# A delta-rule attention block followed by a two-layer PReLU feed-forward, one core: VectorE's weight differences and block-inversion pieces of chunks two to four dealt out anew, and one step's late transposes issued one group earlier

## The chip, the cores and the metric

The kernel runs on one core of one Trainium2 chip. That core has five engines that run side by side, each taking its own instructions in order: TensorE (PE in the profile: matmuls and transposes; PEld is its weight load), VectorE (DVE), ScalarE (ACT), GpSimd (POOL) and SyncE (SP, which here only issues DMAs). Engines wait for one another through semaphores. The metric is the device time of one execution in microseconds (us); lower is better.

## The reference

Four batches, eight heads, 768 tokens, head size 48. For each head a 48 x 48 state runs over the tokens; its outputs, laid side by side, are the 384 inputs of a feed-forward with 2048 inner units.

```python
k_n = k / (np.linalg.norm(k, axis=-1, keepdims=True) + 1e-06)
for t in range(S):
    y[:, :, t] = einsum('bhd,bhde->bhe', q[:, :, t], state)
    v_old = einsum('bhde,bhd->bhe', state, k_n[:, :, t])
    state = state + beta[:, :, t] * einsum('bhd,bhe->bhde', k_n[:, :, t], v[:, :, t] - v_old)
x = y.transpose(0, 2, 1, 3).reshape(B * S, H * D)      # 3072 x 384
h = x @ w_in                                           # 384 -> 2048
g = np.maximum(h, 0.0) + alpha * np.minimum(h, 0.0)
out = g @ w_out                                        # 2048 -> 384
```

## The kernel before

**Chunks and steps.** The tokens are cut into 12 chunks of 64. A chunk holds 256 tokens over the four batches. The attention of one chunk is done in two *steps*, one for each pair of batches, so there are 24 steps, n = 0 to 23; step n belongs to chunk n // 2. Inside a chunk the recurrence is solved as a triangular system: a Gram matrix of the keys (`grams`, L495), the inverse of a unit triangular matrix, a product with the state (`through_state`, L793), the solve with the inverse (`solve`, L824, whose result `u` VectorE scales at L831), the outputs (`outputs`, L836) and the new state (`next_state`, L853).

**Block inversion.** The 32 x 32 diagonal blocks of four steps at a time are inverted together on VectorE by `eliminate` (L578). Such a job has 39 pieces (`WHOLE`, L619): four transposes in, one piece for GpSimd, 30 elimination pieces of one product (L593) and one addition (L599), and two times four transposes out (`back`, L605), of which the last four write `inverse`. ScalarE's `placing` (L693) puts the result where the step's matmuls read it (L704, L707). `between` (L749) makes the off-diagonal part on TensorE (L733), and ScalarE copies it back (L745).

**Feed-forward.** `ffn_in` (L989) makes the 2048 inner units of a chunk in eight groups of six matmuls (L998; each shows as two records in the trace). A group fills one PSUM bank; ScalarE takes the negative part out of it (L1008) and VectorE adds the scaled parts with two instructions (L1010), after which the bank is free. Up to step 8 there are only two such banks (`ps_ffn`, L101), so group i + 2 cannot begin before L1010 of group i has ended. From chunk 2 on the second layer is `ffn_out_fast` (L1051), a scheme with seven block products instead of eight (L1062). It needs four sums of the activations in each of two halves (`operand_sums`, L943, VectorE L952) and, once for the whole kernel, four differences of blocks of `w_out` in each of two halves: `weight_sums(b, first, last)` (L970), eight instructions of 128 x 768 values at L985. The first three differences of a half go to spare memory, the fourth overwrites a block of `w_out` itself and is needed only by the last of the seven products. The plain second layer of chunk 1, `ffn_out(1)` (L1028, matmuls L1041), still reads `w_out` as it was.

**Who orders the work.** Every engine's order is written out by hand. `weave` (L1376) takes generators, each with a number of pieces and a place from which it starts, and lets them advance in proportion; `part(g, n)` takes the next n pieces of a generator. Steps 4 and 5 are each one `weave` (L1913) of `attention(n)` in four groups, `part(late, rest)`, which is the rest of `ffn_out(1)`, and `part(blocks, share)`, pieces of the block inversion for steps 8 to 11. Step 5 also weaves in `weight_sums(0, 0, 3)`. From step 6 (`JOINED`) on a step is three `stretch`es of matmuls of the feed-forward (`tail`), woven with the block pieces that `PIECES_OF` (L1920) deals out and with the extra generators of `extra`. The other five weight differences stand in steps 6 and 7: `weight_sums(1, 0, 3)` in step 6's second stretch, `weight_sums(0, 3, 4)` in its third, `weight_sums(1, 3, 4)` in step 7's first.

**Step 4 and 5's groups.** Group 1 of `attention(n)` is `through_state`, a mask (L521), `between_1`; group 2 `solve`, `grams`, `between_2`; group 3 `outputs`, `next_state` and the squares of a later step's keys (ScalarE L388, VectorE L392); group 4 `flips` (L440), `to_ffn` (L901), the norm's root and reciprocal (ScalarE L407 and L408, VectorE L412) and loads. `flips` turns a later step's keys and queries round with eight TensorE transposes (L429) into a pair of PSUM banks, from which ScalarE copies them (L455, L457). `to_ffn` does the same with the step's outputs (L908, L910).

**Three PSUM pairs in turn.** `ps_big` (L77) hands out three pairs of banks round and round. So in step 5 `solve` reuses the pair of `through_state`, which the mask L521 reads last; `flips` reuses the pair of `between_2`, which the copies L745 read last; and step 6's `through_state` reuses the pair of `flips`, which L457 reads last.

Of the kernel before, what the change touches and what calls it, by code (L numbers as in the profile page):

```python
# [36 lines left out]
EARLY = 8  # L37
# [7 lines left out]
def kernel(  # L45
# [31 lines left out]
    def ps_big():  # L77

        big.append(big.pop(0))
        return big[-1]  # L80
# [313 lines left out]
    def squares(n):  # L394
        if n < N:
            squared(n)
            norms(n)
# [42 lines left out]
    def flips(n_k, n_q):  # L440

        both = n_k < N and n_q < N
        p = ps_big() if both else None
        copies = []
        if n_k < N:
            p_k = p[:, 0] if both else ps_one()
            flip(early(n_k), p_k)
            k_t[n_k] = work.tile([128, G, 128], FP32, name="k_t", bufs=EARLY + 1)
            copies.append((k_t[n_k], p_k))
        if n_q < N:  # L450
            p_q = p[:, 1] if both else ps_one()
            flip(q_pad[n_q % NQ], p_q)
            q_t[n_q] = beside[steps[n_q][1]][:, :, :, D : D + C]
        for dst, src in copies:
            nc.scalar.copy(dst.rearrange("p g i -> p (g i)")[0:ROWS], src[0:ROWS])  # L455
        if n_q < N:
            nc.scalar.copy(  # L457
                q_t[n_q].rearrange("p t g i -> p g t i")[0:ROWS],
                p_q.rearrange("p (g t i) -> p g t i", g=G, t=2)[0:ROWS],
            )  # L460
# [67 lines left out]
    NJ = 4  # L528
# [192 lines left out]
    PLACING = 3  # L721
# [246 lines left out]
    summed = []  # L968
# [82 lines left out]
    def ffn_out_fast(c):  # L1051


        gss.pop(c)
        later = operand_sums(1)
        o = [work.tile([128, DM], FP32, name="o_sb") for _ in range(2)]
        left, right_ = slice(0, DM // 2), slice(DM // 2, DM)
        u = [work.tile([128, DM // 2], FP32, name=f"u{i}", bufs=1) for i in (2, 3)]

        def some(p, x, w, which):  # L1060
            for i in which:
                nc.tensor.matmul(p, x(i), w(i), start=(i == 0), stop=(i == FP - 1))  # L1062
                if i % 2 == 1:
                    next(later, None)
                    if i < FP - 1:
                        yield

        def product(x, w):
            p = ps_ffn()[:, 0 : DM // 2]
            yield from some(p, x, w, range(FP))  # L1070
            return p

        def operand(f, u):
            return lambda i: act[:, i, f, u * 128 : (u + 1) * 128]

        def sum_(x):
            return lambda i: sums[:, i, x]

        def weight(f, v):
            return lambda i: w_half[:, i, f, v]  # L1080

        def w_sum_(x):
            return lambda i: w_sum(i, x)

        def add(to, x, p):
            nc.vector.tensor_tensor(out=to, in0=x, in1=p, op=ALU.add)

        if len(ffn_banks) > 2:
            a, b = (
                (ps_ffn()[:, 0 : DM // 2], operand(f, 0), weight(f, 0)) for f in range(2)  # L1090
            )
            yield from some(*a, range(FP - 2))
            yield from some(*b, range(FP - 2))
            yield from some(*a, range(FP - 2, FP))
            nc.scalar.copy(u[0], a[0])
            yield
            yield from some(*b, range(FP - 2, FP))
            add(o[0][:, left], u[0], b[0])
            yield
        else:  # L1100
            p = yield from product(operand(0, 0), weight(0, 0))
            nc.scalar.copy(u[0], p)
            yield
            p = yield from product(operand(1, 0), weight(1, 0))
            add(o[0][:, left], u[0], p)
            yield
        for _ in later:
            assert False
        assert summed.count(0) == summed.count(1) == 4
        p = yield from product(sum_(1), w_sum_(1))  # L1110
        add(u[0], u[0], p)
        yield
        p = yield from product(lambda i: act[:, i, 0, 128:256], w_sum_(2))
        add(u[1], u[0], p)
        yield
        p = yield from product(sum_(0), w_sum_(0))
        add(o[0][:, right_], u[0], p)
        add(o[1][:, right_], u[1], p)
        yield
        p = yield from product(sum_(2), weight(1, 1))  # L1120
        add(o[0][:, right_], o[0][:, right_], p)
        store(c, 0, o[0])
        yield
        p = yield from product(operand(1, 1), w_sum_(3))
        add(o[1][:, left], u[1], p)
        store(c, 1, o[1])
        yield
# [243 lines left out]
    def part(gen, n):  # L1371
        for _ in range(n):
            next(gen, None)
            yield
# [18 lines left out]
    def attention(n):  # L1393

        assert n + EARLY + 1 < TURNED_K
        now(through_state(n))
        now(between_1(n + 1))
        yield
        now(solve(n))
        now(grams(n + EARLY))  # L1400
        now(between_2(n + 1))
        scale_v(n + 1)
        yield
        now(outputs(n))
        now(next_state(n))
        load_late(n + 2)
        squares(n + EARLY + 1)
        yield
        flips(n + EARLY + 1, n + 2)
        to_ffn(n)  # L1410
        if n < JOINED - 1:
            place(n + 2, (0,))
        now(weigh(n + EARLY + 1))
        if n == JOINED - 1:
            load_early(TURNED_K)
        load_q(n + 3)
        load_v(n + 3)
        yield

    WY, JOINED = G * D, NJ + 2  # L1420
# [196 lines left out]
    n = 2 * W_IN_P  # L1617
# [16 lines left out]
    def chain(*gens):  # L1634
        for g in gens:
            yield from g
# [92 lines left out]
    n = 12  # L1729
# [114 lines left out]
    n = WHOLE + PIECES - BEGUN - SOON  # L1844
# [31 lines left out]
    n = OUT_PARTS - few - 2 * rest + 1  # L1876
# [30 lines left out]
        gens += [(part(blocks, share), share, 0.3), (each(later), len(later), soon)]  # L1907
        weave(*[x for x in gens if x[1] > 0])

    share = 9  # L1910
    for n in range(NJ, JOINED):
        extra = [] if n == NJ else [(weight_sums(0, 0, 3), 3)]
        weave(  # L1913
            (attention(n), SHARES), (placing(n + 1, (1, 2, 3)), SHARES * PLACING),
            (part(late, rest), rest),
            (part(blocks, share), share), *extra,
        )
# [11 lines left out]
    for n in range(JOINED, N):  # L1929
        if n == NARROW:  # L1930
            banks(2, 2)
        fill, share = FILL.get(n, FILLS[n % 2]), PIECES_OF.get(n, TURNS[n % NJ])
        extra = [[], [], []]
        if n == JOINED:
            place(n + 1, (0,))
            extra[1] = [(weight_sums(1, 0, 3), 3)]
            extra[2] = [(weight_sums(0, 3, 4), 1)]
        elif n == JOINED + 1:
            extra[0] = [(weight_sums(1, 3, 4), 1, 0.6), (placing(n + 1, (1, 2, 3)), PLACING)]

        later = burst_a(n)
        if is_turned(n - 1):
            if n % 2:
                rows = rows_y(n - 1)
                extra[1].append((part(rows, 8), 8))
                extra[2].append((part(rows, 8), 8, 0.3))
            else:
                extra[0].append((rows_y(n - 1), 16, 0.4))
        stretch(
            fill[0], blocks, share[0], later, *extra[0], *put_off, soon=0.5 if n == JOINED else 0.0  # L1950
        )
        put_off = []
        later = turn_round(n)
        if n == JOINED:
            extra[1].append((placing(n + 1, (1, 2, 3)), PLACING))
        stretch(fill[1], blocks, share[1], later, *extra[1], soon=0.2)
        m, ends = (n + 6) // NJ, n % NJ == 2
        if ends and n > JOINED:
            for _ in blocks:
                assert False  # L1960
            place(n + 2, (0,))
        later = burst_b(n) + [lambda: scale_v(n + 1)]
        if NARROW <= n < N - 2:
            later.append(lambda: turn_q(n + 2))
        if n == JOINED:
            stretch(fill[2], blocks, share[2], later, *extra[2])
            for _ in blocks:
                assert False
            place(n + 2, (0,))
            place(n + 3, (0,))  # L1970
            blocks = eliminate(m)
        else:
            if ends:
                blocks = eliminate(m) if m < N // NJ else iter(())
            after = [(placing(n + 2, (1, 2, 3)), PLACING)]
            if n % NJ != 1:
                after.append((placing(n + 3, (0,)), 1))
            if n >= LATE:
                put_off, after = after, []
            stretch(  # L1980
                fill[2], blocks, share[2], later, *after, *extra[2], soon=0.1 if n >= LATE else 0.5
            )
# [34 lines left out]
```

## Time and profile before

| what | value |
| --- | --- |
| three runs | 643.0 us median (642.51 to 644.19) |
| profiled execution, its own time | 643.5 us |
| span of the profile | 641.8 us |
| granted TensorE clock | 1.0 of full speed |
| PE busy over 155 to 208 us | close to all of it, with five waits listed |
| weight differences L985 | 8 x 0.95 us, at 165.0, 169.9, 173.6, 183.0, 185.7, 187.6, 190.7 and 202.1 us |

Rows of the timeline read: start (us from the span's start), duration (us), engine, line, operation, output<-input, size, count, and in brackets how long the engine had been idle and what released it. Two neighbouring rows may overlap: an engine starts the next instruction while the former still drains. So the distance from one start to the next is what a row costs on its engine. A row with a count merges several instructions.

Steps stand in this profile at about these times: step 4 from 146 us, step 5 from 160, step 6 from 173.5, step 7 from 194.5, step 8 from 219.

### The profile page before, as it was taken

The numbers are of one execution on the slowest core, as the hardware profiler recorded it, in microseconds if no ns is written. First come the engines' busy times: TensorE is split into PE (matmuls) and PEld (weight loads), VectorE is DVE, ScalarE is ACT, GpSimd is POOL, SyncE is SP. The second block draws the span as 40 slices with busy tenths as digits, with TensorE's granted clock in tenths as the row PEclk, the third lists the DMA queues.
The fourth block names the chain that finished last, engine by engine and source line by source line (L and its number), as shares of the span: only waits on it lengthen the run. The fifth ranks groups of instructions, "written<-read, shape, count | busy, mean of one in ns | idle before, by whom it ended". The sixth has DMA issues, their size and how long they took to land.

```text
span 641.8 us, 21687 instructions
## 1 busy us (share of the span) xinstructions
PE 627.9 (98%) x9154; PEld 552.0 (86%) x9154; DVE 500.8 (78%) x1213; ACT 309.9 (48%) x816; POOL 92.4 (14%) x204
## 2 busy tenths in 40 slices
PE   6999999999999999999999999999999999999997
PEld 4587887566787988988988988988999999999997
DVE  4976988977999889859879858968979569477383
ACT  5887664344454243644643735435447356353230
POOL 6001211000000100001000000000044053061350
PEclk9999999999999999999999999999999999999999
DMA  7957835311343143143143122121121310100000
GB/s 118 300 129 167 237 66 141 82 28 37 56 77 57 30 74 53 27 77 52 26 75 52 25 50 31 33 45 26 32 47 27 54 26 6 36 1 2 26 1 26
DMA packets 145969, 39.27 MB, mean 61 GB/s; under 512 B 139040, under 2 KB 142256, under 8 KB 145872
## 3 DMA queue, kind: packets, MB, share of 16 engines
q1 hardware_dynamic: 144000, 37.40, 28.5%
q8 instruction: 72, 1.18, 0.7%
q10 hardware_dynamic: 1872, 0.49, 0.4%
q14 instruction: 25, 0.20, 0.1%
HBM read 33.14 MB, written 4.72 MB: 59 GB/s over the span
## 4 chain that ended last, share of the span: by engine, by line
PE 82%; DVE 10%; ACT 2%; DMA 2%; issue 1%; SPq 1%; POOL 1%; ACTq 0%; DVEq 0%; POOLq 0%
PE p_ffn L998 11%; PE p_ffn L1062 9%; PE p_more L1331 8%; PE p_more L1062 8%; PE p_more L998 7%; PE p_ffn L1041 7%; PE p_more L1247 4%; PE p_ffn L1237 3%; PE p_ffn L1331 3%; PE p_ffn L1242 2%; PE p_pair L733 2%; PE p_pair L802 2%; PE p_pair L1508 2%; PE p_pair L840 2%; PE p_pair L501 2%; DVE act L1010 2%
## 5 line engine op out<-in xcount | busy, mean ns | idle before, releaser
L998 PE MATMUL p_ffn<-xt,w_in 128*128 128x256 f32 x528 | 124.1, 384 | 1.3 <-ACT space_out L263 0.4
L998 PEld LDWEIGHTS p_ffn<-xt,w_in 128*128 128x128 f32 x528 | 97.4, 190 | 16.3 <-issue 1.6
L896 ACT COPY xt<-z 32x96 f32<-32x96 f32 x240 | 64.5, 269 | 48.5 <-DVE z L883 45.4
L998 PE MATMUL p_more<-xt,w_in 128*128 128x256 f32 x240 | 55.7, 382 | 0.0
L599 DVE TENSOR_TENSOR block<-block,prod 128x30 f32<-128x30 f32 (+9 forms) x150 | 49.8, 332 | 5.2
L1271 POOL TENSOR_TENSOR k_t<-k_t 128x128 f32<-128x128 f32 (+1 forms) x48 | 28.3, 590 | 166.6 <-ACT k_t L1266 164.1
L998 PEld LDWEIGHTS p_more<-xt,w_in 128*128 128x128 f32 x240 | 44.9, 190 | 6.3
L745 ACT COPY inv<-p_pair 32x256 f32<-32x256 f32 x40 | 14.5, 363 | 73.4 <-DVE u L831 40.9
L593 DVE TENSOR_TENSOR prod<-block 128x30 f32<-128x30 f32 (+9 forms) x150 | 48.7, 325 | 1.1
L418 POOL TENSOR_TENSOR beta_t<-beta_t,rec 128x8 f32<-128x8 f32 x24 | 6.1, 255 | 271.0 <-DVE rec L412 262.0
L1010 DVE SCALAR_TENSOR_TENSOR act<-act,al_t,p_ffn 128x256 f32<-128x256 f32 x72 | 31.1, 473 | 15.9 <-ACT act L1008 15.8
L1008 ACT ACTIVATE act<-p_ffn 128x512 f32<-128x512 f32 x36 | 21.4, 594 | 28.3 <-PE p_ffn L998 28.0
L1271 POOL TENSOR_TENSOR block<-block 128x128 f32<-128x128 f32 (+1 forms) x48 | 27.6, 575 | 12.6 <-ACT block L1266 10.1
L1237 PE MATMUL p_ffn<-xt,w_in 128*128 128x256 f32 x96 | 29.3, 387 | 0.0
L1062 PE MATMUL p_ffn<-w_out,act 128*128 128x192 f32 x160 | 28.4, 329 | 0.5 <-DVE act L1010 0.4
L1062 PEld LDWEIGHTS p_ffn<-w_out,act 128*128 128x128 f32 x160 | 26.2, 190 | 1.7 <-DVE act L1010 0.8
L831 DVE TENSOR_TENSOR u<-p_pair,wgt 128x384 f32<-128x384 f32 x24 | 13.2, 554 | 16.6 <-PE p_pair L827 10.1
L1010 DVE SCALAR_TENSOR_TENSOR act<-act,al_t,p_more 128x256 f32<-128x256 f32 x40 | 17.3, 474 | 10.9 <-ACT act L1008 10.8
L812 DVE TENSOR_TENSOR r<-v_raw,p_pair 64x192 f32<-64x192 f32 (+1 forms) x66 | 23.2, 352 | 2.3 <-PE p_pair L802 1.2
L554 ACT COPY same<-right 32x256 f32<-32x256 f32 x29 | 11.7, 402 | 22.7 <-DVE right L507 19.1
L1062 PE MATMUL p_more<-w_out,act 128*128 128x192 f32 x128 | 22.3, 326 | 0.0
L1041 PE MATMUL p_ffn<-w_out,act 128*128 128x384 f32 x64 | 21.8, 491 | 0.4 <-DVE more L1010 0.4
(256 smaller groups left out, 1472.8 us busy)
## 6 DMA issues: line engine op xcount, KB each, us to landing
w_out<-in_moe_w_in_dram SPq DMA_DIRECT2D x10, 512.0 KB, 5.3
v_raw<-in_v_dram SPq DMA_DIRECT2D x48, 96.0 KB, 2.7
kl<-in_k_dram SPq DMA_DIRECT2D x96, 48.0 KB, 2.5
out_dram<-o_sb SPq DMA_DIRECT2D x90, 48.0 KB, 1.6
space_out<-in_moe_w_out_dram SPq DMA_DIRECT2D x11, 384.0 KB, 4.3
ke_last<-in_k_dram SPq DMA_DIRECT2D x25, 96.0 KB, 3.3
qp<-in_q_dram SPq DMA_DIRECT2D x64, 32.0 KB, 2.2
w_out<-in_moe_w_out_dram SPq DMA_DIRECT2D x5, 384.0 KB, 4.3
```

What stands on the lines that cost most here:

```text
L593: nc.vector.tensor_tensor(out=prod, in0=r[:, 0:j, j : j + 1].to_broadcast([128, j, n]), in1=r[:, j : j + 1, j + 1 : HB].to_broadcast([128, ...
L599: nc.vector.tensor_tensor(out=r[:, 0:j, j + 1 : HB], in0=r[:, 0:j, j + 1 : HB], in1=prod, op=ALU.add)
L812: nc.vector.tensor_tensor(out=r[to, a], in0=v_in[to, a], in1=p[own, a, :, 0:D], op=ALU.subtract)
L896: nc.scalar.copy(to[quad(r), u, bp, t], z[quad(2 * t + u), r])
L998: nc.tensor.matmul(p_h[:, i], w_in[:, t, (f + i) * 128 : (f + i + 1) * 128], xt[:, t], start=(t == 0), stop=(t == KT - 1),)
L1010: nc.vector.scalar_tensor_tensor(out=g[:, i], in0=g[:, i], scalar=al_t[:, f + i : f + i + 1], in1=p_h[:, i], op0=ALU.mult, op1=ALU.add,)
L1041: nc.tensor.matmul(p_o[u], gs[f // 2][:, f % 2, u * 128 : (u + 1) * 128], w_out[:, f], start=(f == 0), stop=(f == FT - 1),)
L1062: nc.tensor.matmul(p, x(i), w(i), start=(i == 0), stop=(i == FP - 1))
L1237: nc.tensor.matmul(p[:, f * 256 : f * 256 + 256], w(2, f), xt[:, 2], start=True, stop=False)
L1247: nc.tensor.matmul(q[:, j], a, b, start=True, stop=True)
L1271: nc.gpsimd.tensor_tensor(out=dst, in0=a, in1=b, op=ALU.add)
L1331: nc.tensor.matmul(p, x(i), w(i), start=(i == 0), stop=(i == FP - 1))
```

## The change

Four edits. Line numbers in this document are those of the kernel before.

1. The three differences `weight_sums(0, 0, 3)` move from step 5 to step 4.
2. `share`, the block pieces of steps 4 and 5, goes from 9 to 10 in each. The number of pieces in step 6's second stretch is worked out from `share`, and falls from 4 to 2.
3. `weight_sums(1, 0, 3)` begins in the first stretch of step 6 with one difference and has its other two in the second. The two last differences, of both halves, move into the third stretch of step 7. An assertion in `ffn_out_fast` that all eight have been issued moves behind the first products accordingly.
4. In step 5 alone `flips` is issued with group 3, ahead of the `yield`, and not with group 4. Between the two groups stand three matmuls of `ffn_out(1)`.

```diff
@@ ffn_out_fast
-        assert summed.count(0) == summed.count(1) == 4
+        assert summed.count(0) >= 3 and summed.count(1) >= 3
         p = yield from product(sum_(1), w_sum_(1))
...
+        assert summed.count(0) == summed.count(1) == 4
         p = yield from product(operand(1, 1), w_sum_(3))
@@ attention
         squares(n + EARLY + 1)
+        if n == JOINED - 1:
+            flips(n + EARLY + 1, n + 2)
         yield
-        flips(n + EARLY + 1, n + 2)
+        if n < JOINED - 1:
+            flips(n + EARLY + 1, n + 2)
         to_ffn(n)
@@ steps 4 and 5
-    share = 9
+    share = 10
     for n in range(NJ, JOINED):
-        extra = [] if n == NJ else [(weight_sums(0, 0, 3), 3)]
+        extra = [(weight_sums(0, 0, 3), 3)] if n == NJ else []
@@ steps 6 and 7
         if n == JOINED:
             place(n + 1, (0,))
-            extra[1] = [(weight_sums(1, 0, 3), 3)]
-            extra[2] = [(weight_sums(0, 3, 4), 1)]
+            own = weight_sums(1, 0, 3)
+            extra[0] = [(part(own, 1), 1, 0.5)]
+            extra[1] = [(part(own, 2), 2)]
         elif n == JOINED + 1:
-            extra[0] = [(weight_sums(1, 3, 4), 1, 0.6), (placing(n + 1, (1, 2, 3)), PLACING)]
+            extra[0] = [(placing(n + 1, (1, 2, 3)), PLACING)]
+            extra[2] = [(chain(weight_sums(0, 3, 4), weight_sums(1, 3, 4)), 2)]
```

Set side by side, the two built programs hold the same instructions on every engine. ScalarE, GpSimd and SyncE have them in the same order. On TensorE one thing moves: the eight transposes of step 5's `flips` stand ahead of three matmuls L1041 that they followed. On VectorE the order differs from step 4's sixth elimination piece to the second elimination piece of the next block inversion, which stands at 214.3 us in the profile before:

| place on VectorE | before | after |
| --- | --- | --- |
| step 4 | 9 pieces of the block inversion | 10 pieces, three L985 |
| step 5 | 9 pieces, three L985 | 10 pieces |
| step 6, from L507's end to the first L1010 | 2 pieces | 2 pieces, one L985 |
| step 6, from there to the fourth L1010 | 4 pieces, three L985 and the first that overwrites `w_out` | 3 pieces, two L985 |
| step 7, ahead of the mask L521 | the second L985 that overwrites `w_out` | none |
| step 7, from L507's end to the third elimination piece of the next block inversion | none | both L985 that overwrite `w_out` |

## The prediction

> **What bounds the kernel now.** I read the page first: its first part and the chain that ended last.
>
> ```profile
> PE 627.9 (98%) x9154; PEld 552.0 (86%) x9154; DVE 500.8 (78%) x1213; ACT 309.9 (48%) x816; POOL 92.4 (14%) x204
> ...
> PE 82%; DVE 10%; ACT 2%; DMA 2%; issue 1%; SPq 1%; POOL 1%; ACTq 0%; DVEq 0%; POOLq 0%
> ```
>
> TensorE sets the end; VectorE holds only a tenth of the chain. In the chain by time that tenth lies mostly at 184 to 207 and 237 to 257 us; the diff touches 150 to 214 us. So I read TensorE's timeline there, and the chain for its pace when nothing is late.
>
> ```profile
> 289.15 5.18 PE p_more L998 x24
> ```
> ```profile
> 172.66 0.81 PE L1041 MATMUL p_ffn<-w_out,more 128*128 128x384 f32 x2
> 173.66 1.00 PE L802 MATMUL p_pair<-beside,k_t 48*64 48x112 f32 x32 [0.19 <-ACT beside L457]
> ...
> 180.36 1.89 PE L998 MATMUL p_ffn<-xt,w_in 128*128 128x256 f32 x8
> 182.69 3.88 PE L998 MATMUL p_ffn<-xt,w_in 128*128 128x256 f32 x16 [0.43 <-DVE act L1010]
> 186.50 0.69 PE L501 MATMUL p_pair<-k_t 48*64 48x64 f32 x32
> ...
> 196.63 4.58 PE L998 MATMUL p_ffn<-xt,w_in 128*128 128x256 f32 x20
> 201.76 0.55 PE L908 MATMUL p_pair<-ident,y 128*128 128x128 f32 x3 [0.54 <-ACT mid L745]
> 202.14 2.76 PE L998 MATMUL p_ffn<-xt,w_in 128*128 128x256 f32 x12
> 205.14 2.51 PE L1062 MATMUL p_ffn<-w_out,act 128*128 128x192 f32 x14 [0.24 <-DVE act L1010]
> 207.82 1.96 PE L1062 MATMUL p_ffn<-w_out,act 128*128 128x192 f32 x10 [0.17 <-DVE act L1010]
> ```
>
> The bracketed idle times add to 1.57 us. I price by starts instead, since the ends are modelled. L998 at full pace costs 5.18 / 24 = 0.216 us, L1062 0.1625 (the chain's 5.20 for 32), L1041 0.34 (six from 169.41 to 171.45 in the same timeline); a run that follows or precedes small matmuls costs about 0.1 more at that end.
>
> - A: 182.69 and the rest to 186.50: 6.14 us for 24 L998 against 5.18 + 0.09: 0.87 lost.
> - B: 201.76: 5.13 for 20 against 4.32 + 0.2: 0.6.
> - C: 205.14: 3.00 for 12 against 2.59: 0.4.
> - D: 207.82: 2.68 for 14 against 2.28: 0.4.
> - E: 173.66: 1.00 for two L1041 against 0.7: 0.3.
>
> Together 2.57 us. That is all the change can win here. A, C and D wait for VectorE's L1010; B for ScalarE, which had itself waited for VectorE:
>
> ```profile
> 198.78 0.51 ACT L704 ACTIVATE inv<-inverse,which 128x256 f32<-128x256 f32 x1 [3.04 <-DVE inverse L566]
> ...
> 200.96 0.74 ACT L745 COPY mid<-p_pair 32x256 f32<-32x256 f32 x2
> ```
>
> The Trainium skill ("Trainium Kernel Development and Optimization", Performance Expectations, "Reading a trace") calls matmul busy time a bad metric, as matmuls are pipelined. The rows agree: 1.57 by idle, 2.57 by starts. By idle alone the sum below would be 641.8.
>
> **Part 1: three L985 and one piece into step 4.** VectorE had room there:
>
> ```profile
> 155.25 0.55 DVE L849 TENSOR_TENSOR y<-y,p_pair 128x384 f32<-128x384 f32 x1 [0.55 <-PE p_pair L840]
> ...
> 160.84 0.20 DVE L412 RECIPROCAL rec<-norm 128x8 f32<-128x8 f32 x1 [2.47 <-ACT norm L408]
> ...
> 165.02 0.95 DVE L985 TENSOR_TENSOR space_out<-w_out 128x768 f32<-128x768 f32 x1
> 165.89 0.40 DVE L593 TENSOR_TENSOR prod<-block 128x240 f32<-128x240 f32 x1
> ```
>
> An L985 costs 0.87 from start to start. A piece's addition is followed 0.44 later by the next piece, which needs it, but 0.32 later by an independent row (164.70 to 165.02), so each L985 between two pieces costs about 0.77. Laying the new order over the old starts: `u` (L831) 151.48 to 152.27 (TensorE's L840 needs it at 154.50), L849 155.25 to 156.25 (L908 at 158.50), then 867 and 392, two pieces, the third L985 at 159.29, the extra piece, and L412 at 160.86 instead of 160.84. The room of 3.02 is used up to the last 0.02. Cost 0.02, and none to spare: behind L412 stand L812 and the mask L521 of step 5, and the solve already waits for that mask:
>
> ```profile
> 164.40 0.56 PEld L827 LDWEIGHTS p_pair<-r,inv 64*64 64x64 f32 x32 [0.60 <-DVE a_t L521]
> ```
>
> Every us that VectorE comes later to L412 is a us of TensorE at L827. Bounds: VectorE 0.3 earlier gains 0.06 (the L1041 before it hide the rest); 0.3 later costs 0.3. I take 0.02.
>
> The skill ("VectorE: DVE Perf Modes", Terms, DRAIN) says the next VectorE operation cannot issue until the pipe is empty. The rows disagree: the piece behind the L985 starts 0.08 before its recorded end. By the rule the three would cost 0.24 more, and the sum 641.1.
>
> **Part 2: step 5 without L985.** Behind the mask two L985 (1.6) leave ahead of `right` (L507) or L849, and a piece (0.8) comes: L831 167.54 to 166.8, L507 168.33 to 167.6, L849 171.49 to 170.0.
>
> **Part 3: `flips` one group earlier.** Eight L429, no DMA of their own; their keys and queries landed long before (issues at 124 and 159.4 to 161.7, landing 3.7 at most). They move past three L1041 (2.04), to 169.41. Their banks are free only when `between_2`'s L745 has ended: before at 170.35, behind L554, which waited for L507. With L507 0.73 earlier L745 ends at 169.62. So TensorE, which runs through at 169.41 before, waits about 0.26; bounds: 0 (L507 1 us earlier) and 0.94 (not earlier at all). Behind the wait stand the three L1041 and L908, which nobody misses. In return L457 ends near 171.7, two us ahead of L802, and E goes: -0.3. Step 5 as a whole: +0.02 + 0.26 - 0.3, nothing. The loads that wait for L429 on SyncE's queue come no later.
>
> **Part 4: step 6.** L412 now waits for the norm (174.05 against 175.17) and L812 to L507 run 1.1 earlier. L554 starts at 178.1 (179.24), L388 and the first L1008 at 179.5 (180.62), and the first L1010 ends at 181.3 (182.46), with one L985 ahead of it. TensorE wants the bank at 182.1. The second ends at 184.0 (185.3), wanted at 184.75; its L466 needs `qp`, whose last issue at 179.0 lands by 182.7 at most, at the end of the L985. The third ends at 186.5 (189.3). A goes whole: -0.87.
>
> From L831 on VectorE keeps up with TensorE and so gains no more by waiting: the fourth L1010 at 190.1 (191.64). The rest follows at the old spacing, so the last transpose of `inverse` ends at 197.15 (198.74). L704, the next L1008 (TensorE's group ends 197.8) and four copies put L745's end at 200.36 (201.70), and L908 wants it at 200.3: of B's 0.6 some 0.1 stays. -0.5. Bounds: 0 to -0.6.
>
> **Part 5: step 7 without the second `w_out` L985.** The next L1010 stands at 201.7 (204.13) against a need at 203.4; the last at 204.9 (207.32), its first half done 205.3 against 205.7. C and D go: -0.8; bounds -0.4 (only C) and -0.8.
>
> **Where the two L985 land.** 0.87 each between 211 and 214 us. Ahead of the first L1086 (213.42 to 212.7, with all else earlier) and the second (215.67 to 213.9). What covers them: before, VectorE was idle 0.94 at 215.67, and TensorE needs the bank that the first L1086 frees only at about 213.3. Cover gone, each costs at most its 0.87.
>
> **Sum.** 0 - 0.87 - 0.5 - 0.8 = -2.2 us. The profiled execution took 643.5 (span 641.8, 1.7 around it), half a us over the median, which is inside the runs' spread; I subtract from the median: 643.0 - 2.2 = **640.8**. Behind 214 us TensorE's order is the same and VectorE has idle spots to fall back in step, so I carry the gain to the end.
>
> **The rivals.** About 0.3% (1.9 us) is what a measurement of this kernel can tell from no change.
>
> - *Half of it is given back in step 5.* VectorE's chain in step 4 is 0.4 longer than I laid it: L827 waits 0.4, L507 comes 0.3 earlier only and `flips` waits 0.65, and B stays with 0.3. -2.2 + 0.4 + 0.4 + 0.2 = -1.2: 641.8. For: the margin of 0.02 comes from eight added starts. Against: those are rows of the same shapes. 0.27.
> - *The wait for the norm stays (slower).* L412 before waited 2.47 for ScalarE. If ScalarE's root comes late by as much as VectorE's L392 (157.24 instead of 156.24) and what then stands before it, VectorE is idle again with the L985 already spent: 2.9 late at L412 and so at L827. Less the later gains of 2.2 and plus 0.3 at `flips`: 644.0. It decides once L412 starts after 163. Against: L407 started at 160.33, 2.6 after L392's new end, held by L455 to L707 and not by L392. 0.06.
> - *It does nothing:* the waits at A to D are only moved to other groups of the same two banks, since PSUM turn-over and not VectorE's load sets them: 642.7. Against: at 289.15 the same matmuls run without a wait, but with four banks. 0.09.
>
> The forecast has 0.58; its own range is 640.2 to 641.5. Of it some 0.44 lies beyond 1.9 us, so faster 0.46, same 0.49 (0.14 of the forecast, the first and third rival almost whole), slower 0.05. The range of 8 in 10: 639.8 to 642.7.
>
> **What would show it.** Right: TensorE's idle of 0.43 at 182.69 gone, L908 with at most 0.2, no wait for L1010 around 205; L412 of step 5 without idle before it, at 160.8 to 161.0; a new wait of 0.2 to 0.4 of L429 for L745 near 169.5. Wrong: PEld's L827 waiting over 1 us for L521; L429 waiting near 1 us; waits for L1010 at other groups of 176 to 208; TensorE waiting for L1086 after 213.

## The result, and the profile after

| | before | after |
| --- | --- | --- |
| median | 642.51 us (7 runs, 641.62 to 644.19) | 639.87 us (7 runs, 638.53 to 640.89) |
| ratio, 95% interval | | 0.9954 (0.994 to 0.9968) |
| profiled execution, its own time | 643.5 us | 640.03 us |
| its span | 641.8 us | 638.2 us |

The changed kernel is faster: by 2.64 us (0.41%) between the medians, by 0.46% by the ratio of the runs, and the whole interval lies beyond 0.3%. 640.8 was forecast, inside a range of 639.8 to 642.7; the chances given with it put no change (0.49) ahead of faster (0.46).

The first part of the page after, and its chain of waits by engine:

```profile
PE 624.2 (98%) x9154; PEld 550.9 (86%) x9154; DVE 500.4 (78%) x1213; ACT 310.4 (49%) x816; POOL 93.0 (15%) x204
...
PE 87%; DVE 5%; DMA 3%; ACT 2%; SPq 1%; issue 1%; POOL 1%; ACTq 0%; DVEq 0%; POOLq 0%
```

The same instructions ran: VectorE is busy for 500.4 us against 500.8. Its share of the chain fell from 10% to 5%. TensorE's timeline in the stretch that the prediction read:

```profile
168.75 0.65 PE L429 MATMUL p_pair<-ident,ke_last 128*112 128x128 f32 x4 [0.25 <-ACT inv L745]
...
171.94 0.81 PE L1041 MATMUL p_ffn<-w_out,more 128*128 128x384 f32 x2
172.68 1.00 PE L802 MATMUL p_pair<-beside,k_t 48*64 48x112 f32 x32
...
179.30 5.34 PE L998 MATMUL p_ffn<-xt,w_in 128*128 128x256 f32 x24
184.58 0.69 PE L501 MATMUL p_pair<-k_t 48*64 48x64 f32 x32
...
194.59 4.58 PE L998 MATMUL p_ffn<-xt,w_in 128*128 128x256 f32 x20
199.21 0.55 PE L908 MATMUL p_pair<-ident,y 128*128 128x128 f32 x3
199.59 2.76 PE L998 MATMUL p_ffn<-xt,w_in 128*128 128x256 f32 x12
202.19 4.06 PE L1062 MATMUL p_ffn<-w_out,act 128*128 128x192 f32 x24
```

All five brackets of before are gone; one of 0.25 is new, at L429. Where before broke 24 L998 into 8 and 16 and 24 L1062 into 14 and 10, each is one row now. The list of TensorE's waits between 155 and 265 us says the same:

```profile
PE p_ffn L998 <- issue: 0.4, 1, 0.4
PE p_pair L429 <- ACT inv L745: 0.2, 1, 0.2
```

The first of these stands at 231.84 and was there before, at 235.36.

**Where the time came from.** I call *window* the time on TensorE from the first L802 of step 5 to the first L501 of step 7, which follows the L1062: 160.21 to 209.71 before, 159.30 to 206.18 after. All that the diff moves takes effect inside it, but for the two late L985. (VectorE does three L985 ahead of it now, in step 4, but TensorE's step 4 takes 13.68 after and 13.69 before.) From row start to row start:

| from, to (start before) | before | after | change | forecast |
| --- | --- | --- | --- | --- |
| step 5: L802 to L802 of step 6 (160.21) | 13.45 | 13.38 | -0.07 | 0 |
| A: L802 to L501 (173.66) | 12.84 | 11.90 | -0.94 | -0.87 |
| L501 to L998 x20 (186.50) | 10.13 | 10.01 | -0.12 | 0 |
| B: L998 x20 and L908 (196.63 to 202.14) | 5.51 | 5.00 | -0.51 | -0.5 |
| C and D: L998 x12 and L1062 (202.14) | 7.57 | 6.59 | -0.98 | -0.8 |
| window | 49.50 | 46.88 | -2.62 | -2.2 |

Of A's row, 0.86 lies in the 24 L998 themselves (6.14 to 5.28). The other 0.09 lies at the head of step 6, between L784 and L733 (0.65 before, 0.56 after). In all ten kernels of this document it is 0.56 where `flips` comes early and 0.64 or 0.65 (174.47 to 175.12 before) where it does not, so it belongs to edit 4.

Behind the window, up to the end of SyncE's last instruction, the two profiled executions agree to 0.02 us (432.02 and 432.00). Ahead of it they differ by 0.91, and 0.92 of difference is there already at the program's first L802 (57.41 and 56.49 us), long before anything that was edited. So -2.62 is the change's own. The medians' -2.64 agrees with it, but its interval is about 2.1 to 3.9 us, so that the last digits agree is luck.

### The profile page after: what moved, and what is told of

It reads as the page before. It is cut to its first block, busy times and chain, and to the rows that moved or that the text cites. A ratio compares the mean times of both kernels' runs of the same rounds, so it can differ in the third digit from the quotient of the medians.

```text
span 638.2 us, 21687 instructions
## 1 busy us (share of the span) xinstructions
PE 624.2 (98%) x9154; PEld 550.9 (86%) x9154; DVE 500.4 (78%) x1213; ACT 310.4 (49%) x816; POOL 93.0 (15%) x204
## 4 chain that ended last, share of the span: by engine, by line
PE 87%; DVE 5%; DMA 3%; ACT 2%; SPq 1%; issue 1%; POOL 1%; ACTq 0%; DVEq 0%; POOLq 0%
PE p_ffn L998 14%; PE p_ffn L1062 9%; PE p_more L1332 8%; PE p_more L1062 8%; PE p_more L998 7%; PE p_ffn L1041 6%; PE p_more L1248 4%; PE p_ffn L1238 3%; PE p_ffn L1332 3%; PE p_pair L802 3%; PE p_ffn L1243 3%; PE p_pair L733 2%; PE p_pair L840 2%; PE p_pair L501 2%; PE p_pair L1512 2%; PE p_pair L827 2%
## 5 line engine op out<-in xcount | busy, mean ns | idle before, releaser
L998 PE MATMUL p_ffn<-xt,w_in 128*128 128x256 f32 x528 | 123.4, 384 | 1.5 <-ACT space_out L263 1.0
L998 PEld LDWEIGHTS p_ffn<-xt,w_in 128*128 128x128 f32 x528 | 97.7, 190 | 15.4 <-ACT space_out L263 1.1
L998 PE MATMUL p_more<-xt,w_in 128*128 128x256 f32 x240 | 55.7, 382 | 0.0
L998 PEld LDWEIGHTS p_more<-xt,w_in 128*128 128x128 f32 x240 | 44.9, 190 | 6.3
L1010 DVE SCALAR_TENSOR_TENSOR act<-act,al_t,p_ffn 128x256 f32<-128x256 f32 x72 | 31.0, 472 | 17.1 <-ACT act L1008 17.1
L1062 PE MATMUL p_ffn<-w_out,act 128*128 128x192 f32 x160 | 28.0, 327 | 0.0
L1062 PEld LDWEIGHTS p_ffn<-w_out,act 128*128 128x128 f32 x160 | 26.3, 190 | 0.6 <-DVE act L1010 0.3
L1010 DVE SCALAR_TENSOR_TENSOR act<-act,al_t,p_more 128x256 f32<-128x256 f32 x40 | 17.3, 473 | 10.9 <-ACT act L1008 10.8
L812 DVE TENSOR_TENSOR r<-v_raw,p_pair 64x192 f32<-64x192 f32 (+1 forms) x66 | 23.2, 352 | 2.3 <-PE p_pair L802 1.2
L1062 PE MATMUL p_more<-w_out,act 128*128 128x192 f32 x128 | 22.3, 326 | 0.0
L1041 PE MATMUL p_ffn<-w_out,act 128*128 128x384 f32 x64 | 21.8, 491 | 0.4 <-DVE more L1010 0.4
L554 ACT COPY same<-right 32x256 f32<-32x256 f32 x29 | 11.7, 403 | 21.2 <-DVE right L507 17.7
```

The source lines that it names most:

```text
L812: nc.vector.tensor_tensor(out=r[to, a], in0=v_in[to, a], in1=p[own, a, :, 0:D], op=ALU.subtract)
L998: nc.tensor.matmul(p_h[:, i], w_in[:, t, (f + i) * 128 : (f + i + 1) * 128], xt[:, t], start=(t == 0), stop=(t == KT - 1),)
L1010: nc.vector.scalar_tensor_tensor(out=g[:, i], in0=g[:, i], scalar=al_t[:, f + i : f + i + 1], in1=p_h[:, i], op0=ALU.mult, op1=ALU.add,)
L1041: nc.tensor.matmul(p_o[u], gs[f // 2][:, f % 2, u * 128 : (u + 1) * 128], w_out[:, f], start=(f == 0), stop=(f == FT - 1),)
```

## The experiments

Whole times of these kernels scatter by up to six us from run to run, so a cause worth 0.5 us can't be read from them. The window can, though it is one profiled execution each: kernels whose timelines show the same waits have windows within 0.1 us of each other. So the expectations were put on the window, and the times stand beside it. The diffs leave out assertions. The first four kernels ran on one chip (before there: 642.76, median of 24 runs), the other four on another (642.16 of 22).

| kernel | window | median time | ratio, 95% interval |
| --- | --- | --- | --- |
| before | 49.50 | | |
| the change | 46.88 | 639.87 | 0.9954 (0.994 to 0.9968) |
| flips alone | 49.50 | 643.09 | 1.0004 (0.9991 to 1.0018) |
| all but flips | 46.97 | 640.59 | 0.9974 (0.9956 to 0.9991) |
| edits 1 and 2 | 47.86 | 640.75 | 0.9969 (0.9956 to 0.9981) |
| edit 3 | 47.91 | 640.99 | 0.9969 (0.9957 to 0.9981) |
| share 9 | 46.88 | 640.25 | 0.996 (0.9947 to 0.9973) |
| one more in step 4 | 47.75 | 640.5 | 0.9966 (0.9954 to 0.9978) |
| flips one matmul later | 46.61 | 639.9 | 0.9958 (0.9944 to 0.9972) |
| no differences | 46.98 | 639.25 | 0.9945 (0.9925 to 0.9966) |

**1. `flips` alone moved up.** Before, with edit 4 only.

```diff
         squares(n + EARLY + 1)
+        if n == JOINED - 1:
+            flips(n + EARLY + 1, n + 2)
         yield
-        flips(n + EARLY + 1, n + 2)
+        if n < JOINED - 1:
+            flips(n + EARLY + 1, n + 2)
```

> Before, with step 5's flips one group earlier and nothing else. Window W = start of step 5's first L802 to start of step 7's first L501: 49.50 us in the profile before, 46.88 in the changed one. Theory (flips pays by itself in a wait for L745, and the later waits for L1010, which VectorE sets on its own, swallow what step 5 loses): L429 waits about 1.0 us for L745 (end 170.35 in the profile before), the wait of 0.3 at L802 goes, step 5 is 0.7 longer, and the waits at step 6's third L998 group shrink by the same 0.7: W 49.3 to 49.7, time as before. Rival (the costs add): W 50.2. Rival (flips earlier is what pays): W below 49.0.

The window is 49.50, as before, and the time can't be told from before's. TensorE's rows with a bracket in this kernel, those of L1062 left out:

```profile
171.62 0.65 PE L429 MATMUL p_pair<-ident,ke_last 128*112 128x128 f32 x4 [0.91 <-ACT inv L745]
...
202.98 0.55 PE L908 MATMUL p_pair<-ident,y 128*128 128x128 f32 x3 [0.54 <-ACT mid L745]
```

`flips` waits 0.91 for the banks of `between_2`: the prediction's upper bound for the case that L507 comes no earlier was 0.94. That pushes step 6 back by 0.67 (14.12 for the first row of the table above against 13.45). VectorE, which is not pushed back, catches up, so A's bracket goes: its 24 L998 take 5.56, against 6.14 before and 5.28 in the change. The same loss has changed its place.

**2. The change without edit 4.**

```diff
         squares(n + EARLY + 1)
-        if n == JOINED - 1:
-            flips(n + EARLY + 1, n + 2)
         yield
-        if n < JOINED - 1:
-            flips(n + EARLY + 1, n + 2)
+        flips(n + EARLY + 1, n + 2)
```

> The changed kernel with flips back in its old place. Theory: L802 of step 6 waits again for L457, 2.2 us behind the start of flips as before, which makes up exactly for the wait of 0.25 at L429 that goes: W 46.8 to 47.1, time as the changed kernel's (639.9). Rival (flips earlier is needed for the rest, because step 6 starts earlier): W 47.3 or more and waits for L1010 come back.

46.97: without edit 4 the window is 0.09 longer than the change's. E's wait of 0.19 for L457 is back and the 0.25 at L429 is not there. In step 5 the two cancel, as Part 3 of the prediction had it (13.36 here, 13.38 in the change). The 0.09 is the one between L784 and L733, which Part 3 did not have. So moving `flips` is worth a tenth of a us. The median, 640.59, lies 0.7 above the change's, but these twelve runs go from 638.38 to 644.73, so that says nothing about it.

**3. Edits 1 and 2 alone.** The three L985 in step 4, `share` 10; steps 6 and 7 as before.

```diff
-    share = 9
+    share = 10
     for n in range(NJ, JOINED):
-        extra = [] if n == NJ else [(weight_sums(0, 0, 3), 3)]
+        extra = [(weight_sums(0, 0, 3), 3)] if n == NJ else []
```

> Three L985 in step 4 and ten pieces in steps 4 and 5, all else as before. Theory (VectorE's lateness in steps 5 and 6 is what most of the waits come from): the waits at step 6's third group and at L908 go, those before the L1062 stay by the second L985 that overwrites w_out, 0.87 late: W 47.2 to 47.9, some 2.0 us under before. Rival (each edit pays for its own step only): W 48.6, since only A goes.

47.86, at the upper edge. A and B are gone, two waits of 0.17 for L1010 in front of L1062 stay, and so does E's.

**4. Edit 3 alone.** The three L985 stay in step 5; in step 6 one L985 stands ahead of the first L1010, and both that overwrite `w_out` are in step 7's last stretch.

```diff
-            extra[1] = [(weight_sums(1, 0, 3), 3)]
-            extra[2] = [(weight_sums(0, 3, 4), 1)]
+            own = weight_sums(1, 0, 3)
+            extra[0] = [(part(own, 1), 1, 0.5)]
+            extra[1] = [(part(own, 2), 2)]
         elif n == JOINED + 1:
-            extra[0] = [(weight_sums(1, 3, 4), 1, 0.6), (placing(n + 1, (1, 2, 3)), PLACING)]
+            extra[0] = [(placing(n + 1, (1, 2, 3)), PLACING)]
+            extra[2] = [(chain(weight_sums(0, 3, 4), weight_sums(1, 3, 4)), 2)]
```

> The five L985 of steps 6 and 7 dealt out as in the change, those of step 5 left there, nine pieces, flips late. Theory: the L985 that comes ahead of step 6's first L1010 makes its wait 0.87 longer (1.3 idle instead of 0.43), the waits at L908 and before both L1062 go: W 48.6 to 49.4, some 0.5 us under before. Rival (the two L985 out of step 7 are what pays): W 48.0 or less. Rival (it is a loss by itself): W over 49.5.

47.91: my theory missed, and so low a window is what the first rival gave. It had the L985 ahead of the first L1010 lengthen A's wait by its 0.87; the wait is 0.43, to the digit what it was:

```profile
181.63 3.88 PE L998 MATMUL p_ffn<-xt,w_in 128*128 128x256 f32 x16 [0.43 <-DVE act L1010]
```

VectorE's timeline shows why, first before's, with the earlier rows left out:

```profile
180.63 0.55 DVE L392 TENSOR_REDUCE norm<-ksq 128x8 f32<-128x384 f32 x1 [0.82 <-ACT ksq L388]
...
181.67 0.86 DVE L1010 SCALAR_TENSOR_TENSOR act<-act,al_t,p_ffn 128x256 f32<-128x256 f32 x2
```

and this kernel's, which runs 1.05 us earlier by the clock of its own span:

```profile
178.68 0.95 DVE L985 TENSOR_TENSOR more<-w_out 128x768 f32<-128x768 f32 x1
179.58 0.55 DVE L392 TENSOR_REDUCE norm<-ksq 128x8 f32<-128x384 f32 x1
...
180.62 0.87 DVE L1010 SCALAR_TENSOR_TENSOR act<-act,al_t,p_ffn 128x256 f32<-128x256 f32 x2
```

Before, VectorE stood idle for 0.82 in front of L392, waiting for ScalarE's squares L388, which stand behind L554, which waits for VectorE's L507. The L985 fills just that hole, and L1010 starts 5.93 us after the step's first L501 in both (181.67 - 175.74, 180.62 - 174.69). So A is named after L1010, but at this place it is not set by what VectorE has to do there. It is set by how late L507 is (the second of the two, which writes `right`): it starts 3.04 after that L501 before and 3.05 here, 2.05 with edits 1 and 2, 1.75 in the change (176.43 - 174.68). What makes L507 late is step 5's three L985. L412, which precedes it on VectorE, starts without idle time in front of it before and here, and after a wait for ScalarE's norm with edits 1 and 2. Before, then edits 1 and 2:

```profile
175.17 0.19 DVE L412 RECIPROCAL rec<-norm 128x8 f32<-128x8 f32 x1
```
```profile
174.31 0.20 DVE L412 RECIPROCAL rec<-norm 128x8 f32<-128x8 f32 x1 [0.57 <-ACT norm L408]
```

Taking them out removes A (experiment 3, and experiment 5 without the tenth piece); easing step 6 does not (this one).

Set side by side, the two halves divide the rest. C and D go with edit 3: from the L998 x12 to L501 it takes 6.61 here and 7.50 with edits 1 and 2 (7.57 before). B is won by either, and so is the 0.1 between L501 and the L998 x20: the halves shorten the window by 1.64 and 1.59 alone and by 2.53 together (experiment 2), 0.70 less than the sum. From step 7's first L802 to L908 both take what the change takes, 6.58 and 6.59 against 7.09 before.

**5. The change with `share` 9.**

```diff
-    share = 10
+    share = 9
```

> The changed kernel with nine block pieces in steps 4 and 5 instead of ten, so four instead of two in step 6's second stretch. Theory (in step 5 VectorE's L412 is held by ScalarE's norm, not by the pieces ahead of it): VectorE is idle about 1.0 us before L412 instead of 0.19 and everything behind it stands as before; the two pieces more in step 6 fit into its idle 1.07 and 1.32 there: W 46.8 to 47.1, L429's wait 0.25 as in the changed kernel. Rival (the tenth piece is needed, or costs): W off by 0.3 or more either way.

46.88, as in the change. VectorE waits 1.07 in front of L412, as expected. Behind the window, at 257.41, L1062 waits 0.29 for L1010, but the wait at 231.74 is about as much shorter, 0.16 against 0.42, so nothing is lost. The tenth piece brings nothing that can be seen. (Between the first and the fourth L1010 of step 6 the trace of before has five pieces, not the four of the table of the change.)

**6. One more L985 in step 4.** The first difference is computed twice.

```diff
-        extra = [(weight_sums(0, 0, 3), 3)] if n == NJ else []
+        extra = [(chain(weight_sums(0, 0, 1), weight_sums(0, 0, 3)), 4)] if n == NJ else []
```

> The changed kernel with the first weight difference computed twice, so four L985 in step 4; the fourth comes to stand behind step 5's L412. Theory (no room is left there: a us later at the mask L521 is a us of TensorE at L827): L827 waits 0.8 longer and nothing gives it back: W 47.5 to 47.8. Rival (other slack takes it up): W under 47.1.

47.75, 0.87 longer, and it is the wait that the prediction named as the one without room. VectorE's timeline of this kernel, then TensorE's:

```profile
159.77 0.20 DVE L412 RECIPROCAL rec<-norm 128x8 f32<-128x8 f32 x1
159.89 0.91 DVE L985 TENSOR_TENSOR space_out<-w_out 128x768 f32<-128x768 f32 x1
```
```profile
164.22 0.68 PE L827 MATMUL p_pair<-r,inv 64*64 64x48 f32 x32 [0.88 <-DVE a_t L521]
```

The fourth L985 falls behind L412, ahead of L812 and the mask, and TensorE pays it whole at the solve. So there is no room behind L412; ahead of it the change left 0.19.

**7. `flips` one matmul later.** An L1041 goes ahead of it, so that the wait of 0.25 at L429 should go.

```diff
-        if n == JOINED - 1:
-            flips(n + EARLY + 1, n + 2)
         yield
...
+    def turned_round(n):
+        flips(n + EARLY + 1, n + 2)
+        yield
+
     share = 10
     for n in range(NJ, JOINED):
-        extra = [(weight_sums(0, 0, 3), 3)] if n == NJ else []
+        extra = [(weight_sums(0, 0, 3), 3)] if n == NJ else [(turned_round(n), 1, 0.55)]
```

> The changed kernel with step 5's flips one matmul L1041 later (one ahead of it, two behind, instead of three behind). Theory: L745 has ended by then, L429's wait of 0.25 idle (0.32 to 0.46 by starts) goes and L457 is still 1.4 us ahead of L802: W 46.4 to 46.6, the lowest of all. Rival (TensorE is held by something else at that place): W 46.8 to 46.9.

46.61, a hundredth over the range, the shortest of all, with no wait left in the window. Between 155 and 265 us TensorE's list has only the one at 231 us, which is there in before too:

```profile
PE p_ffn L998 <- issue: 0.5, 1, 0.5
```

So what the window of before loses to waits, with and without a bracket, is nearer 2.9 us (49.50 - 46.61) than the 2.57 of the prediction. But 0.27 us of 640 can't be seen in the times: 639.9 stands beside the change's 639.87, which was measured apart.

**8. None of the eight differences.** Before, without L985. The memory for the differences is set to zero by GpSimd instead, and the differences that the second layer reads are left out of the computation.

```diff
+    nc.gpsimd.memset(more, 0.0)
...
-            nc.vector.tensor_tensor(out=dst, in0=x, in1=y, op=ALU.subtract)
```

> Before, with all eight weight differences left out (the second layer from chunk 2 on then uses wrong sums of w_out; their spare memory is zeroed by GpSimd at the start instead). It shows what the eight L985 cost in all in their old places, and what is left to win. Theory (the waits A to D are VectorE's load and nothing else): no wait for L1010 between 176 and 208 us, L802's wait of 0.3 for L457 stays, W 46.8 to 47.1: the change has taken all there was. Rival (the two PSUM banks' turn-over sets a part): waits for L1010 stay, W 47.5 or more. Rival (the change has left something): W under 46.6.

46.98. The waits of TensorE between 155 and 265 us in this kernel:

```profile
PE p_ffn L998 <- issue: 0.4, 1, 0.4
PE p_pair L802 <- ACT beside L457: 0.2, 1, 0.2
```

Only E is left, which is about `flips`. With seven us of VectorE's work deleted (8 x 0.87) TensorE gains 2.52; experiment 2, which leaves `flips` in its old place too, gains 2.53 by dealing the same work out elsewhere. There is nothing more to be had from these instructions.

## Why the prediction was right, and where it was wrong

**What bounds it: right in place, too small in size.** The prize lay where the prediction looked, but it was not "all the change can win". 2.57 by starts was priced on the five stretches at a bracket, and every other row was put at full pace without a look. The change made the window 2.62 shorter although it pays 0.27 for the new wait at L429 (step 5 takes 13.38, and 13.11 in experiment 7), and experiment 7, without that wait, made it 2.89 shorter. That 2.62 lies so near 2.57 is luck. What had been put at nothing: about 0.18 in the ten L1062 behind the second bracket of D, 0.11 in the 24 L998 ahead of L840 in step 6, 0.09 between L784 and L733 in step 6, and 0.08 in front of L859 and of what follows it in step 5. Less the 0.1 of B that stays and the 0.04 by which E was priced too high, that makes up the difference. Brackets alone, 1.57, would have been further off still. The Trainium skill ("Trainium Kernel Development and Optimization", Performance Expectations, "Reading a trace") calls the busy time of matmuls a bad metric for how close a kernel is to roofline. The profile agrees: by its page TensorE is busy for 98% of the span before and after.

**Part 1, step 4: right.** L412 was laid at 160.86 against 160.84. After, it stands at 159.93, which is 160.84 on before's clock (the 0.91 ahead of the window added). VectorE's timeline after, with the third L985, and the load of the solve's weights:

```profile
158.04 0.95 DVE L985 TENSOR_TENSOR space_out<-w_out 128x768 f32<-128x768 f32 x1
...
159.93 0.20 DVE L412 RECIPROCAL rec<-norm 128x8 f32<-128x8 f32 x1 [0.19 <-ACT norm L408]
```
```profile
163.51 0.56 PEld L827 LDWEIGHTS p_pair<-r,inv 64*64 64x64 f32 x32 [0.62 <-DVE a_t L521]
```

VectorE was even 0.2 ahead of what was laid, so that L412 waited 0.19 for ScalarE's norm, where the prediction's sign was no idle time at all. The solve waits for the mask 0.62 against 0.60. The price of 0.87 per L985 from start to start holds: a fourth one cost 0.87.

The Trainium skill ("VectorE: DVE Perf Modes", Terms, DRAIN) would have had the next operation wait until the pipe is empty; the same page of the Trainium skill adds, under "The DRAIN you can't avoid", that a next operation that is not held starts earlier. The rows are with the addition: the L985 at 158.04 ends at 158.99 by its record, and the next row starts at 158.91.

**Parts 2 and 3, step 5: right.** A wait of 0.25 at L429 against 0.26, and 0.74 for the two L1041 in front of L802 against 1.00 before (171.94 to 172.68): E was 0.26 rather than 0.3, and with it came the 0.09 between L784 and L733, which had been put at nothing. Step 5 as a whole -0.07 instead of 0: the wait and E cancel to 0.01, and 0.08 goes in front of L859 and of the row behind it. Experiment 1 shows the bound that was given for the wait without an earlier L507.

**Part 4, step 6: right.** A went whole: its 24 L998 gave 0.86, and 0.87 was forecast. L507 comes 1.29 earlier against L501 instead of 1.1. Experiments 3 and 4 show that A's gain comes from step 5's L985, as Part 4 had it. The four copies behind `inverse`, on ScalarE after:

```profile
196.12 0.51 ACT L704 ACTIVATE inv<-inverse,which 128x256 f32<-128x256 f32 x1 [3.07 <-DVE inverse L566]
...
198.42 0.74 ACT L745 COPY mid<-p_pair 32x256 f32<-32x256 f32 x2
```

The second ends at 199.16; L908 starts at 199.21 without a bracket. L998 x20 with its end now costs 4.62 (194.59 to 199.21), against 4.52 by the prediction's prices: B's tenth that stays. It is not the weight differences' doing, as it is 4.61 without any (experiment 8). Not forecast was -0.12 between L501 and the L998 x20. It lies in the 24 L998 that follow L733, 5.49 before (188.20 to 193.69) and 5.38 after (186.28 to 191.66), and 5.37 in experiment 8. So the weight differences cost it; that it was a wait too short for a bracket is likely, but no row shows one.

**Part 5, step 7: right in kind, too small in size.** C gave its 0.4 (3.38 to 2.98 from L908 to L1062). D was priced on the 14 L1062 of the row with the bracket of 0.24 alone, 2.68 against 2.28. The 10 behind the second bracket were slow as well: 24 L1062 took 4.57 before and take 3.99 now. D was 0.58, not 0.4. This is the term that was mis-sized most, by 0.18; with step 5, the row of A and the L998 x24 (0.07, 0.07 and 0.12) it makes up the difference between 2.2 and 2.62.

**Where the two L985 land: right.** VectorE's timeline after:

```profile
209.89 1.15 DVE L985 TENSOR_TENSOR w_out<-w_out,space_out 128x768 f32<-128x768 f32 x1
210.96 0.34 DVE L1086 TENSOR_TENSOR o_sb<-u,p_ffn 128x192 f32<-128x192 f32 x1
...
212.05 0.95 DVE L985 TENSOR_TENSOR w_out<-w_out,more 128x768 f32<-128x768 f32 x1
212.92 0.34 DVE L1086 TENSOR_TENSOR u<-u,p_ffn 128x192 f32<-128x192 f32 x1
```

The first L1086 comes 4.78 after step 7's L501 (206.18) instead of 3.71 (213.42 - 209.71), the idle 0.94 in front of the second is used up, and no matmul waits for either.

**The base.** 643.0 was the median of three runs; that of seven is 642.51. Of the 0.93 between 640.8 and 639.87, 0.49 is the base and 0.44 the sum.

**The rivals, and the step that failed.** *Half given back in step 5* fell: the solve's wait grew by 0.02 and `flips` waited 0.25, not 0.65. *The wait for the norm stays* fell: ScalarE's L407 starts at 159.43, 160.34 on before's clock against 160.33, with VectorE's L392 0.67 later than before (156.00, or 156.91 on before's clock, against 156.24): L392 does not hold it. *It does nothing* fell: no wait for L1010 is left between 176 and 208, and experiment 8 shows that the weight differences did set A to D. What failed is the step "Together 2.57 us. That is all the change can win here", and with it the terms of the sum. Rows without a bracket were put at nothing, and D was sized at 0.4 where it was 0.58, so the sum came to 2.2 instead of 2.62. That decided the weighing: 640.8 lay only 0.3 us beyond the bound of 0.3%, so 0.14 of the forecast's 0.58 was put within it, 0.27 went to the first rival for its margin of 0.02, and 0.09 to the third. So no change stood ahead of faster. The margin deserved less doubt: it was a sum of rows of the same shapes on the same engine, and it came true within 0.2 us. Of the priced terms A came out as forecast, B and C too, D above it, and E 0.04 below.

## What to carry to other kernels

Price a wait by the distance between row starts against the same matmuls at full pace, over all the rows up to the next engine's work and not only the one with the bracket: the brackets here held 1.57 of some 2.9 us. Then go through the rows without a bracket the same way: here they held close to half a us. Where a wait is named after an instruction, follow that engine back to its own idle time before moving work: A was named after L1010, but it was set by three weight differences a step earlier, and one put right in front of it cost nothing. And lay the moved work over the old starts, find the one place without room, and trust that sum: here it held to 0.2 us, and one more instruction behind it cost its full 0.87.

## What the runs showed that I had not expected

Nearly all of the scatter between these ten profiles lies ahead of step 5. From the span's start to the first L802 of step 5 the ten profiled kernels took 157.58 to 161.42 us, and three of them whose work up to there is the same took 159.16 (edit 3 alone), 160.21 (before) and 161.42 (flips alone); from step 7's first L501 to the end of SyncE's last instruction all ten took 431.99 to 432.10. At the first L802 of the program they already lie 2.0 us apart (56.4 to 58.4), though not in the same order. The granted clock doesn't order them: it was 0.87 over the first 20 us of the change's profile and 1.00 in before's, whose front is 0.91 longer. What sets it stays open; it was not tried. It means that a change of this size is seen in a window of the trace to a tenth of a us, and in the time only after several runs.
